# A gated convolution block on one core: a listed order of work against one made by a list scheduler, with the windowed convolution in 128x64 tiles

## The chip, the cores and the metric

One core of one Trainium2 chip. The metric is device time in microseconds of the whole program; the kernel before takes 413.35 us, the median of three runs (411.96, 413.48, 413.35).

## What is computed

The input x is 8 sequences of 4224 tokens by 192 channels, float32. Two stages follow each other:

```python
# stage 1: per head (8 heads of 24 channels) a causal window of 7 tokens, weights softmaxed
w = softmax(weight)                                   # 8 x 7
y[b, s, h, :] = sum_k w[h, k] * xpad[b, s + k, h, :]
# stage 2: a gate and two projections
gate = sigmoid(sum_k conv_w[k] * ypad[:, k:k + S, :]) # 5 taps per channel
out = (gate * (y @ w_val)) @ w_out                    # 192 x 192 each
```

The weights `w_val`, `w_out` and `conv_w` arrive as float64 and are turned into float32 on the chip.

## The kernel before

**Blocks and groups.** The host lays the 8 padded sequences out as two streams of 16,936 tokens. Each token block ("step") has 486 or 488 tokens of both streams; there are 35 steps, the last of 380. A group is what the convolution makes at once: 4 steps (two in the first group, one in the last), ten groups (`NJS`, `BLOCKS`).

**Stage 1** runs on TensorE as a matmul with a banded 128x122 matrix per head (`band`): the stationary operand is a 128-token window of x for 128 (segment, channel) pairs, the result 122 tokens of them (`conv_begin`, L294, 424 matmuls in 106 units). Every float32 matmul counts as two instructions in the trace. `conv_end` copies a unit from PSUM to an `e` tile on ScalarE (L309), and a DMA on SP's queue (L313) moves its rows to where stage 2 wants them: channels on partitions, tokens along the row, tiles `x1` (128 channels of each of the two streams, so units 0 and 1) and `x2` (64 channels of both streams, unit 2).

**Stage 2**, per step and for three units: tap 0 on ScalarE into PSUM (L341), four taps on VectorE (L351), sigmoid on ScalarE (L358). The products use float32r in three passes, high part times high, low times high, high times low: the high part is a cast on ScalarE (L373), the low part a subtraction on GpSimd (L376). The product V = `w_val` has parts 12 (128x64 tiles, float32, L422), 21 (64x128 tiles, L431), 11 and 22 (128x128 tiles, L439, L447). VectorE multiplies V into the gate (L469, `gated`), the gated value is split in the same way, and O = `w_out` runs the same four parts. ScalarE copies the three results out (L476) and SP's queue stores them (L480).

**The order.** Every engine's order is written out: `SCHEDULE` lists what one window of two steps does (for instance `T12+0`: tap 2 of unit 1 of this step; `U`, `K`: begin and end of a convolution unit), and `window(n)` walks through it. The code at the end runs 18 convolution units before the first two steps are complete, and a few more in the first windows.

Of the kernel before, what the change touches and what calls it, by code (L numbers as in the profile page):

```python
# [27 lines left out]
NJS = [2] + [4] * 8 + [1]  # L30
# [22 lines left out]

C1, C2 = 16, 8


class Plan:


    def __init__(self, nj):  # L60
        self.nj = nj
        self.segs = (8, 8 if nj % 2 == 0 else 4)
        self.wins = (nj, nj // 2 if nj % 2 == 0 else nj)
        self.rows = (128, 16 * self.segs[1])
        self.off = (0, 128 * nj)
        self.width = 192 * nj
        per = [MB // (WIN * w) for w in self.wins]
        self.units = []
        for h in range(NH):
            for i in range(2):  # L70
                if (h + 1) % per[i] == 0:
                    self.units.append((i, tuple(range(h + 1 - per[i], h + 1))))


PLANS = [Plan(nj) for nj in NJS]
GROUP = [max(1, 4 // nj) for nj in NJS]
# [5 lines left out]
SCHEDULE = """  # L82
    V12+0 T11+0 CG2-1 T04+0 E2-2 O12-1 GL2-1 T12+0 Z2+1 V21+0 T13+0 S2+0 GL0-1 O21-1 CX2+1 T21+1
    CG1-1 T14+0 V22+0 GL1-1 T22+1 V110+0 S0+0 G2+0 V111+0 XL2+1 Z1+1 T23+1 O22-1 CX1+2 G0+0 O110-1
    XL1+1 T24+1 E2-1 O111-1 T11+1 CG0+0 U0 Z0+1 G1+0 U1 T12+1 K0 GL0+0 E0-1 T01+1 U2 K1 T13+1 E1-1
    U3 T02+1 K2 U4 T14+1 K3 T03+1 CG2+0 U5 Z2+2 GL2+0 T04+1 V110+1 K4 T21+2 CG1+0 V111+1 K5 T22+2
    GL1+0 V22+1 Z0+2 T23+2 O22+0 CX1+3 XL1+2 T01+2 O110+0 S2+1 T02+2 O111+0 S0+1 T24+2 V21+1 CX2+2
    T03+2 O21+0 Z1+2 XL2+2 G0+1 V12+1 G1+1 E0+0 CG0+1 O12+0 E1+0 G2+1
"""
SCHEDULE = [re.fullmatch(r"([A-Z]+)(\d*)([+-]\d+)?", t).groups() for t in SCHEDULE.split()]  # L90
SCHEDULE = [(k, a, int(b or 0)) for k, a, b in SCHEDULE]

XW = 768
XBUFS = 8
# [3 lines left out]
def kernel(  # L98
# [17 lines left out]
    op = ctx.enter_context(tc.tile_pool(name="op", bufs=2))
    ps_g = ctx.enter_context(tc.tile_pool(name="ps_g", bufs=2, space=PSUM))
    ps_v = ctx.enter_context(tc.tile_pool(name="ps_v", bufs=6, space=PSUM))

    w0 = cp.tile([128, KW], F32, name="w0")
    scr = [op.tile([128, 3 * MB], F32, tag="ot", name=f"scr_{i}") for i in range(2)]
    scr.append(pp.tile([128, 2, MB], F32, tag="h", name="scr_2").rearrange("p a t -> p (a t)"))
    scr.append(pp.tile([128, 2, MB], F32, tag="l", name="scr_3").rearrange("p a t -> p (a t)"))
    scr_at = [0] * len(scr)

    def scratch(n, i):
        o = scr_at[i]
        scr_at[i] += n  # L130
        return scr[i][:, o : o + n].bitcast(I32)

    raw = {}
    for name, ap, n, i in (("cw", cw, 2 * KG, 0), ("wv", wv, 2 * D, 0), ("wo", wo, 2 * D, 1)):
        t = scratch(2 * n, i)
        raw[name] = t.rearrange("p (n w) -> p n w", w=2), t, ap.bitcast(I32)

    heads = [(g, h) for g in range(NG) for h in range(0, NH, GROUP[g])]
    xtiles, xoff, loaded = {}, {}, [0]
    o = 0  # L140
    for g, h in heads:
        xoff[g, h] = o
        o += WK * PLANS[g].width * GROUP[g]

    def load_x(k=1):
        for _ in range(k):
            i = loaded[0]
            if i == len(heads):
                return
            loaded[0] += 1  # L150
            g, h = heads[i]
            n = PLANS[g].width * GROUP[g]
            t = xin.tile([WK, XW], F32, tag="x", name=f"x_{g}_{h}")
            nc.sync.dma_start(t[:, :n], xw[xoff[g, h] : xoff[g, h] + WK * n].rearrange("(p f) -> p f", f=n))
            for j in range(GROUP[g]):
                xtiles[g, h + j] = t, j * PLANS[g].width

    def load_raw(name):
        nc.sync.dma_start(raw[name][1], raw[name][2])

    RROW = 2 * WIN + KW
    with tc.manual_schedule(engines={ENG.SP}):
        nc.sync.dma_start(w0, hw)
        load_x(2)
        load_raw("cw")
        load_raw("wv")

        one = cp.tile([128, 1], F32, name="one")
        nc.vector.memset(one, 1.0)
        warm = cp.tile([128, 1], F32, name="warm")  # L170
        nc.scalar.activation(warm, one, AF.Exp)
        row = cp.tile([128, RROW], F32, name="row")
        nc.gpsimd.memset(row, 0.0)

        mx = cp.tile([128, 1], F32, name="mx")
        nc.vector.tensor_reduce(out=mx, in_=w0, op=ALU.max, axis=mybir.AxisListType.X)
        w1 = cp.tile([128, KW], F32, name="w1")
        nc.vector.tensor_tensor(out=w1, in0=w0, in1=mx.to_broadcast([128, KW]), op=ALU.subtract)
        w2 = cp.tile([128, KW], F32, name="w2")
        nc.scalar.activation(w2, w1, AF.Exp)  # L180
        warm2 = cp.tile([128, 1], F32, name="warm2")
        nc.scalar.activation(warm2, w2[:, 0:1], AF.Sigmoid)
        sm = cp.tile([128, 1], F32, name="sm")
        nc.vector.tensor_reduce(out=sm, in_=w2, op=ALU.add, axis=mybir.AxisListType.X)
        sm2 = cp.tile([128, 1], F32, name="sm2")
        nc.vector.tensor_scalar(out=sm2, in0=sm, scalar1=1e-9, scalar2=None, op0=ALU.add)
        rs = cp.tile([128, 1], F32, name="rs")
        nc.vector.reciprocal(rs, sm2)
        nc.vector.tensor_tensor(
            out=row[:, WIN - 1 : WIN - 1 + KW], in0=w2, in1=rs.to_broadcast([128, KW]), op=ALU.mult  # L190
        )

        band = cp.tile([WK, NH, WIN], F32, name="band")
        for h in range(NH):
            r = row[16 * h : 16 * h + 1, :]
            src = bass.AP(tensor=r.tensor, offset=r.offset, ap=[list(r.ap[0]), [1, WK], [1, WIN]])
            nc.sync.dma_start(band[:, h, :], src)  # L197
        load_x(2)
        load_raw("wo")
        load_x(3)  # L200
# [386 lines left out]
```

## Time and profile before

| | |
|---|---|
| runs | 411.96, 413.48, 413.35 us, median 413.35 |
| profiled execution | span 411.2 us from its first to its last instruction; a run's own time holds that and 0.8 to 2.3 us around it |
| busy | TensorE 370.8 us, VectorE 350.2, ScalarE 326.3, GpSimd 243.6 |
| DMA | 81.56 MB, mean 198 GB/s |
| TensorE's clock | 0.966 of full speed on average |

A busy time is the union of an engine's instructions; matmuls overlap, so their mean duration is longer than the distance from one to the next. A row's "idle" is the time that the engine stood still just before, with what released it.

### The profile page before, as it was taken

Reading aid. Unit: us, or ns where it says so; the run is one execution under the profiler, and the core shown is the slowest. Engines: PE = TensorE matmul, PEld = TensorE weight load, DVE = VectorE, ACT = ScalarE, POOL = GpSimd, SP = SyncE. Lnnn points to the kernel's source line nnn. Section 1 sums busy time; section 2 is a strip of 40 time slices with the busy share of each in tenths; the row PEclk is TensorE's granted clock in tenths of the full one; section 3 lists DMA queues with packets and bytes.
Section 4 is the critical chain, followed back from the end, with each engine's and each line's share of the span. In section 5 each row is a group of like instructions: output and inputs, shape, how many; then the busy total and the mean of one; then the engine's idle time right before and its main releaser. Section 6 shows DMA issues by size and latency. Waiting matters only on the chain.

```text
span 411.2 us, 7389 instructions
## 1 busy us (share of the span) xinstructions
PE 370.8 (90%) x2458; PEld 296.5 (72%) x2458; DVE 350.2 (85%) x572; ACT 326.3 (79%) x568; POOL 243.6 (59%) x190
## 2 busy tenths in 40 slices
PE   1766367999999999999999999999999999888896
PEld 0666345979797979797979797979797877646564
DVE  4250199979699999999999999999999999999991
ACT  3232538988899899898989898989898989977874
POOL 0220146746377666766676667666757675858582
PEclk9887769999999999999999999999999999999899
DMA  6899990699999996969796969696977824212033
GB/s 140 200 240 225 238 234 20 192 216 276 236 240 291 269 251 236 238 221 214 247 241 217 269 190 266 189 260 208 242 214 200 214 79 135 86 73 120 29 146 129
DMA packets 38806, 81.56 MB, mean 198 GB/s; under 512 B 7280, under 2 KB 25072, under 8 KB 38768
## 3 DMA queue, kind: packets, MB, share of 16 engines
q1 hardware_dynamic: 38512, 80.59, 73.9%
q0 software_dynamic: 256, 0.50, 0.6%
q8 instruction: 19, 0.31, 0.3%
q14 instruction: 19, 0.16, 0.1%
HBM read 28.33 MB, written 26.01 MB: 132 GB/s over the span
## 4 chain that ended last, share of the span: by engine, by line
PE 74%; DMA 10%; DVE 7%; SPq 2%; issue 2%; ACT 2%; POOL 1%; DVEq 0%; POOLq 0%
PE pc L294 21%; PE po L439 10%; PE pv L439 9%; PE pv L431 6%; PE pv L422 6%; PE po L422 6%; PE pv L447 5%; PE po L431 5%; PE po L447 5%; DMA x<-xw 5%; DVE pg L351 4%; DMA x<-e 4%; SPq L197 2%; DVE g L469 2%; POOL pl L376 1%
## 5 line engine op out<-in xcount | busy, mean ns | idle before, releaser
L351 DVE SCALAR_TENSOR_TENSOR pg<-x,cwt,pg 128x486 f32<-128x486 f32 (+2 forms) x315 | 219.6, 723 | 16.2 <-ACT pg L341 13.6
L376 POOL TENSOR_TENSOR pl<-g,ph 128x488 fp32r<-128x488 f32 (+2 forms) x105 | 128.2, 1230 | 99.1 <-ACT ph L373 98.9
L376 POOL TENSOR_TENSOR xl<-x,xh 128x972 fp32r<-128x972 f32 (+3 forms) x70 | 112.4, 1618 | 44.5 <-ACT xh L373 44.5
L294 PE MATMUL pc<-band,x 128*128 128x122 f32 (+1 forms) x848 | 108.2, 289 | 19.6 <-DMA band<-row 9.0
L294 PEld LDWEIGHTS pc<-band,x 128*128 128x128 f32 (+1 forms) x848 | 105.5, 203 | 23.4 <-issue 13.2
L309 ACT COPY e<-pc 128x488 f32<-128x488 f32 x106 | 60.4, 575 | 44.2 <-PE pc L294 25.8
L341 ACT ACTIVATE pg<-x,cwt 128x488 f32<-128x488 f32 (+2 forms) x105 | 70.3, 669 | 14.7 <-DVE g L351 14.7
L351 DVE SCALAR_TENSOR_TENSOR g<-x,cwt,pg 128x488 f32<-128x488 f32 (+2 forms) x105 | 75.0, 715 | 0.7
L469 DVE TENSOR_TENSOR g<-pv,g 128x488 f32<-128x488 f32 (+2 forms) x105 | 67.0, 657 | 9.2 <-PE pv L422 4.2
L373 ACT CAST ph<-g 128x488 fp32r<-128x488 f32 (+2 forms) x105 | 62.6, 597 | 2.6 <-DVE g L469 2.2
L476 ACT COPY ot<-po 128x488 f32<-128x488 f32 (+2 forms) x105 | 59.0, 565 | 6.0 <-PE po L431 3.6
L358 ACT ACTIVATE g<-g 128x486 f32<-128x486 f32 (+2 forms) x70 | 54.8, 808 | 8.6 <-DVE g L351 8.6
L373 ACT CAST xh<-x 128x972 fp32r<-128x972 f32 (+1 forms) x70 | 55.3, 791 | 4.7 <-DMA x<-e 4.2
L422 PE MATMUL po<-g,wof 128*64 128x244 f32 (+2 forms) x280 | 35.0, 368 | 3.4 <-DVE g L469 3.4
L422 PE MATMUL pv<-x,wvf 128*64 128x244 f32 (+2 forms) x280 | 35.9, 378 | 0.5 <-DVE g L469 0.5
L439 PE MATMUL pv<-xl,wvh 128*128 128x486 f32 (+2 forms) x70 | 27.6, 395 | 9.0 <-POOL xl L376 9.0
L422 PEld LDWEIGHTS po<-g,wof 128*64 128x64 f32 x280 | 20.1, 136 | 12.7 <-DVE g L469 4.2
L422 PEld LDWEIGHTS pv<-x,wvf 128*64 128x64 f32 x280 | 18.4, 138 | 14.1 <-issue 4.9
L439 PE MATMUL po<-pl,woh 128*128 128x486 f32 (+2 forms) x70 | 27.4, 391 | 1.2 <-POOL pl L376 1.2
L439 PE MATMUL pv<-xh,wvh 128*128 128x486 f32 (+2 forms) x70 | 28.2, 403 | 0.0
L439 PE MATMUL po<-ph,woh 128*128 128x486 f32 (+2 forms) x70 | 26.8, 383 | 1.3 <-ACT ph L373 1.3
L439 PE MATMUL pv<-xh,wvl 128*128 128x486 f32 (+2 forms) x70 | 26.8, 383 | 0.0
(67 smaller groups left out, 380.6 us busy)
## 6 DMA issues: line engine op xcount, KB each, us to landing
x<-xw SPq DMA_DIRECT2D x70, 384.0 KB, 8.0
x<-e SPq DMA_DIRECT2D x64, 244.0 KB, 7.9
out<-ot SPq DMA_DIRECT2D x18, 729.0 KB, 7.1
out<-ot SPq DMA_DIRECT2D x16, 732.0 KB, 4.6
x<-e SPq DMA_DIRECT2D x72, 122.0 KB, 7.9
out<-ot SPq DMA_DIRECT2D x3, 190.0 KB, 1.9
band<-row SPq DMA_DIRECT2D x8, 61.0 KB, 5.3
x<-e POOLq DMA_DIRECT2D x8, 61.0 KB, 8.1
```

The source lines that it names most:

```text
L294: nc.tensor.matmul(pc[:m, c : c + WIN], lhsT=t[:, o + w * m : o + w * m + m], rhs=band[:, h, :], start=True, stop=True,)
L309: nc.scalar.copy(e[:m, :n], opened.pop((g, u))[:m, :n])
L341: nc.scalar.mul(acc, unit_view(n, i, 0), cwt[:, i // 2, 0:1])
L351: nc.vector.scalar_tensor_tensor(out=dst, in0=unit_view(n, i, k), scalar=cwt[:, i // 2, k : k + 1], in1=acc, op0=ALU.mult, op1=ALU.add,)
L358: nc.scalar.activation(v, v, AF.Sigmoid)
L373: nc.scalar.copy(h, x)
L376: nc.gpsimd.tensor_tensor(out=l, in0=x, in1=h.bitcast(F32), op=ALU.subtract)
L422: nc.tensor.matmul(acc[p, c], lhsT=self.w.f[:, W12 : W12 + 64], rhs=self.x1[:, q, c], start=first and i == 0, stop=not first and i == 1,)
L431: nc.tensor.matmul(acc, lhsT=a[p, W21 : W21 + 128], rhs=b[p], start=first and i == 0, stop=not first and i == 2,)
L439: nc.tensor.matmul(acc, lhsT=a[:, W11 : W11 + 128], rhs=b[:, q], start=first and i == 0, stop=not first and i == 2,)
L469: nc.vector.tensor_tensor(out=v, in0=pvs.pop((n, q)), in1=v, op=ALU.mult)
L476: nc.scalar.copy(ot[:, q * m : (q + 1) * m], pos.pop((n, q)))
```

## The change

The kernel is written anew around the same arithmetic. Nothing of the order is listed any more: the program adds operations with an engine, a cost in ns, dependencies and a priority to a `Scheduler`, whose `run()` makes the order of every engine before the kernel is emitted. Its core, cut:

```diff
-NJS = [2] + [4] * 8 + [1]
-SCHEDULE = """ V12+0 T11+0 CG2-1 T04+0 E2-2 O12-1 ...
+RUNS = [122, 244] + [488] * 16 + [332]
+SPLIT = {122: [240], 244: [484], 488: [486, 486], 332: [484, 176]}
+class Scheduler:
+    SWITCH, STICK = 100, 3500
+    RATE, FLIGHT, LAND = 270.0, 1300, 900
...
+                        k = o.prio + (self.STICK if e == "PE" and mode not in (None, o.mode) else 0)
...
+FULL_OUT = (0,)
+POOL_GATE = (0,)
```
```diff
 convolution of one unit
-    nc.tensor.matmul(pc[:m, c : c + WIN], lhsT=t[:, o + w * m : o + w * m + m], rhs=band[:, h, :], ...)
+    for w, (a, n) in enumerate(cc):
+        for h, P in enumerate(HALVES):
+            nc.tensor.matmul(
+                at(pc)[P, j * run + a : j * run + a + n],
+                lhsT=t[:, off + 128 * w + 64 * h : off + 128 * w + 64 * h + 64],
+                rhs=band[:, head(c, q, h), :n], start=True, stop=True)
+    ns = sum(2 * (0.80 * n + 5) for _, n in cc) * len(qs)
 part 11 of the product O, unit 0 (q in FULL_OUT)
+    nc.tensor.matmul(at(acc[q])[:, :m], lhsT=wf[kind][:, W11 : W11 + 128], rhs=full_x(q), ...)
 gate of unit 0 (q in POOL_GATE)
-    nc.vector.tensor_tensor(out=v, in0=pvs.pop((n, q)), in1=v, op=ALU.mult)
+    nc.scalar.copy(at(vb)[:, :m], at(pv[q])[:, :m])
+    nc.gpsimd.tensor_tensor(out=gate(q), in0=at(vb)[:, :m], in1=gate(q), op=ALU.mult)
 start of the program
-    8 small DMAs make the bands from one row
+    the bands are loaded (500 KB) and exponentiated on ScalarE; 7 matmuls of zeros go first on TensorE
```

In words: (a) groups ("superblocks") of two steps, the first two small (240 and 484 tokens), 19 of them, 36 steps, the last of 176 tokens; the second product's weights are decoded between the first steps' taps. (b) Each convolution matmul has a 128x64 stationary operand, and two heads fill the two column halves of a bank: 848 matmuls, L491. (c) The gate of unit 0 is multiplied on GpSimd from a copy that ScalarE makes (L660, L663); the cast and the subtraction that split it are gone, since (d) part 11 of O for unit 0 is one float32 matmul (L620). (e) Sigmoids are three per step instead of two or three. New lines: taps L578, first split L555 (cast) and L559, gates L669, second split L680 and L684, products L599 (12), L612 (21), L623 (11), L628 (22), copies L505 and L697, row moves L518, loads L475.

**TensorE, middle of the program.** Before (po and pv: results of O and V; pc: a unit of the convolution):

```order
L439 MATMUL po_1_768<-pl_698,woh 128x488
L294 MATMUL pc_9_821<-band,x_6_381 128x122 x4
L294 MATMUL pc_10_829<-band,x_7_591 128x122 x4
L294 MATMUL pc_11_841<-band,x_6_381 128x122 x2
L294 MATMUL pc_11_841<-band,x_7_591 128x122 x2
L294 MATMUL pc_0_854<-band,x_0_593 128x122 x4
L294 MATMUL pc_1_868<-band,x_1_634 128x122 x4
L294 MATMUL pc_2_881<-band,x_0_593 128x122 x2
L294 MATMUL pc_2_881<-band,x_1_634 128x122 x2
L439 MATMUL pv_0_890<-xh_651,wvh 128x488
L439 MATMUL pv_0_890<-xh_651,wvl 128x488
```

All 24 convolution matmuls of two steps stand together, between 128x128 parts. Now (yl, yh, xl, xh: splits of x; ph, pl, ga: the gated value, `bank` any PSUM bank):

```order
L491 MATMUL bank_110<-band,xin_65 64x122 x8
L491 MATMUL bank_109<-band,xin_65 64x122 x8
L599 MATMUL bank_111<-xa_78,wfV 64x242 x2
L599 MATMUL bank_111<-xa_78,wfV 64x244 x2
L628 MATMUL bank_111<-yh_85,whV 128x486
L628 MATMUL bank_111<-yh_85,wlV 128x486
L628 MATMUL bank_111<-yl_86,whV 128x486
L491 MATMUL bank_113<-band,xin_66 64x122 x8
L623 MATMUL bank_112<-xh_83,whV 128x486
L623 MATMUL bank_112<-xh_83,wlV 128x486
L623 MATMUL bank_112<-xl_84,whV 128x486
L620 MATMUL bank_110<-ga_91,wfO 128x486
```

The convolution now stands in pieces of 8 to 24 matmuls, and in these 12 rows the tile form changes three times (128x64, 128x128, 128x64, 128x128). Counted over the whole order, the tile form changes 182 times; before it was 76. Float32 is followed by float32r within 128x128 tiles 29 times, before 15. The last convolution stood 249 rows before TensorE's end, now 108.

**SP's queue, start of the program** (loads x or xin, row moves from e). Before:

```order
L197 DMA band_120<-row_103 128x1x122 x8
L154 DMA x_0_4_129<-xw 128x768
L154 DMA x_0_6_131<-xw 128x768
L159 DMA scr_1_87<-wo 128x768
L154 DMA x_1_0_134<-xw 128x768
L154 DMA x_1_1_136<-xw 128x768
L154 DMA x_1_2_138<-xw 128x768
L313 DMA x1_0_176<-e_0_0_183 16x8x244 x2
L313 DMA x1_0_176<-e_0_1_192 16x8x244 x2
L154 DMA x_1_3_207<-xw 128x768
L154 DMA x_1_4_209<-xw 128x768
L313 DMA x1_0_176<-e_0_3_216 16x8x244 x2
```

Now:

```order
L518 DMA xb0_80<-e0_68 16x4x61 x2
L518 DMA xa0_77<-e1_69 32x4x122
L475 DMA xin3_64<-xw 128x1024
L475 DMA xin4_65<-xw 128x1024
L475 DMA xin5_66<-xw 128x1024
L518 DMA xb1_81<-e2_70 16x4x122 x4
L518 DMA xa1_78<-e3_71 32x4x244
L518 DMA xa1_78<-e4_72 32x4x244
L475 DMA xin6_67<-xw 128x1024
L475 DMA xin0_61<-xw 128x1024
L475 DMA xin1_62<-xw 128x1024
L440 DMA ot0_105<-wo 128x768
```

The rows of the first small superblock are moved (first two rows) before the loads of the third; those loads (xin3 to xin5) then stand ahead of the second superblock's row moves, and the fourth's (xin6, xin0, xin1) ahead of the third's (xb0, xa0).

**GpSimd, from step 4's split on.** Before (xl: low part of x, pl: of the gated value):

```order
L376 TENSOR_TENSOR xl_4_776<-x_1_261,xh_4_775 128x488
L376 TENSOR_TENSOR xl_652<-x_1_260,xh_651 128x976
L376 TENSOR_TENSOR pl_819<-g_3_667,ph_818 128x486
L376 TENSOR_TENSOR pl_3_879<-g_3_668,ph_3_878 128x486
L376 TENSOR_TENSOR pl_819<-g_3_667,ph_818 128x486
L376 TENSOR_TENSOR xl_802<-x_1_260,xh_801 128x2x486
L376 TENSOR_TENSOR xl_5_950<-x_1_261,xh_5_949 128x486
```

Now (gate multiplications are the rows of L663):

```order
L559 TENSOR_TENSOR xl0_84<-xa0_77,xh0_83 128x2x486
L559 TENSOR_TENSOR xl1_88<-xa0_77,xh1_87 128x2x486
L559 TENSOR_TENSOR yl0_86<-xb1_81,yh0_85 128x486
L663 TENSOR_TENSOR ga2_95<-va0_107,ga2_95 128x486
L684 TENSOR_TENSOR pl20_100<-gb2_96,ph20_99 128x486
L684 TENSOR_TENSOR pl10_98<-ga2_95,ph10_97 128x486
L559 TENSOR_TENSOR xl0_84<-xa1_78,xh0_83 128x2x486
L663 TENSOR_TENSOR ga0_91<-va1_108,ga0_91 128x486
```

The multiplication of the gate (ga) stands in the queue behind the splits of later steps, which wait for row moves.

## Rows read from the trace of the kernel before

**Rows 1.** the page: span, then busy time of each engine, share of the span, instructions

```profile
span 411.2 us, 7389 instructions
...
PE 370.8 (90%) x2458; PEld 296.5 (72%) x2458; DVE 350.2 (85%) x572; ACT 326.3 (79%) x568; POOL 243.6 (59%) x190
```

**Rows 2.** stretches: span, busy us of five engines (instructions), PE clock, DMA share, GB/s

```profile
20.00:30.00 10.00, 6.82 (x47) 6.35 (x47) 5.40 (x15) 3.14 (x6) 2.17 (x4) 0.84 1.07 255
50.00:60.00 10.00, 6.23 (x25) 4.07 (x27) 9.75 (x15) 3.74 (x6) 5.27 (x3) 0.54 1.07 220
360.00:380.00 20.00, 17.15 (x96) 10.92 (x94) 19.82 (x32) 15.68 (x26) 14.44 (x11) 1.00 0.22 92
...
157.90:177.87 19.97, 19.97 (x142) 16.35 (x142) 19.34 (x31) 18.29 (x33) 14.27 (x11) 1.00 0.83 230
```

**Rows 3.** PE in order of time, steady part: start us, us, line, operation, count

```profile
157.73 5.51 PE L294 MATMUL pc<-band,x 128*128 128x122 f32 x48
163.01 0.47 PE L439 MATMUL pv<-xh,wvh 128*128 128x488 f32 x1
163.31 0.38 PE L439 MATMUL pv<-xh,wvl 128*128 128x488 f32 x1
163.53 0.38 PE L439 MATMUL pv<-xl,wvh 128*128 128x488 f32 x1
...
170.37 0.99 PE L422 MATMUL pv<-x,wvf 128*64 128x242 f32 x8
171.19 0.99 PE L422 MATMUL po<-g,wof 128*64 128x244 f32 x8
172.11 0.49 PE L431 MATMUL pv<-xh,wvh 64*128 64x486 f32 x2
172.44 0.38 PE L431 MATMUL pv<-xh,wvl 64*128 64x486 f32 x2
...
173.33 0.38 PE L431 MATMUL po<-pl,woh 64*128 64x488 f32 x2
173.63 0.49 PE L447 MATMUL pv<-xh,wvh 128*128 128x486 f32 x1
173.96 0.39 PE L447 MATMUL pv<-xh,wvl 128*128 128x486 f32 x1
...
188.35 0.38 PE L431 MATMUL po<-pl,woh 64*128 64x486 f32 x2
188.66 1.05 PE L422 MATMUL pv<-x,wvf 128*64 128x244 f32 x8
189.54 0.99 PE L422 MATMUL po<-g,wof 128*64 128x242 f32 x8
```

**Rows 4.** groups by line, whole run: busy us, mean ns, idle before

```profile
L376 POOL TENSOR_TENSOR pl<-g,ph 128x488 fp32r<-128x488 f32 (+2 forms) x105 | 128.2, 1230 | 99.1 <-ACT ph L373 98.9
...
L294 PE MATMUL pc<-band,x 128*128 128x122 f32 (+1 forms) x848 | 108.2, 289 | 19.6 <-DMA band<-row 9.0 <-DMA x<-xw 7.3 <-ACT e L309 3.1
...
L469 DVE TENSOR_TENSOR g<-pv,g 128x488 f32<-128x488 f32 (+2 forms) x105 | 67.0, 657 | 9.2 <-PE pv L422 4.2 <-ACT g L358 2.1 <-PE pv L431 1.6
```

**Rows 5.** head: first block of DVE, PE in order of time; a DMA issue, median landing

```profile
49.75 2.26 DVE L351 SCALAR_TENSOR_TENSOR pg<-x,cwt,pg 128x486 f32<-128x486 f32 x3 [8.90 <-ACT pg L341]
...
53.77 0.77 PE L439 MATMUL pv<-xl,wvh 128*128 128x486 f32 x1 [7.28 <-POOL xl L376]
...
71.62 4.57 PE L294 MATMUL pc<-band,x 128*128 128x122 f32 x39
...
x<-e SPq DMA_DIRECT2D x64, 244.0 KB, 7.9
```

**Rows 6.** tail: PE, DVE and ACT in order of time

```profile
337.78 4.09 PE L294 MATMUL pc<-band,x 128*128 128x122 f32 x32
...
403.15 0.55 DVE L469 TENSOR_TENSOR g<-pv,g 128x380 f32<-128x380 f32 x1 [0.39 <-PE pv L422]
...
407.83 0.47 ACT L476 COPY ot<-po 128x380 f32<-128x380 f32 x1 [0.19 <-PE po L439]
```

More of the change, by code (lines that the diff above doesn't have):

```diff
@@ L46 @@
 assert _s == TOTAL
-FLAT = max(s + t for s, t in zip(STARTS, TOKS)) + KW - 1
 N = len(STEPS)
-LAST = N - 1
+TM = max(p.toks for p in SUPERS)
+FLAT = max(p.start + p.toks for p in SUPERS) + WK
 AT = [3 * sum(s[2] for s in STEPS[:n]) for n in range(N + 1)]
[L54 to L72, printed above, removed]
@@ L75 @@
[L75 to L88, printed above, removed]
@@ L89, with head, __init__ @@
[L89 to L94, printed above, removed]
+def head(c, q, half):
+    return 2 * q + half if c == 0 else (q if half == 0 else q + 4)
+class Buf:
+    __slots__ = ("pool", "users", "slot")
+    def __init__(self, pool):
+        self.pool, self.users, self.slot = pool, 0, None
+class Op:
+    __slots__ = ("eng", "ns", "emit", "deps", "prio", "mode", "bufs", "left", "outs", "at", "end", "kb", "ready", "seq", "tag", "chain")
@@ L118 @@
[L118 to L190, printed above, removed]
-        )
[L193 to L200, printed above, removed]
@@ new lines, with at, small, cast_ns @@
+    banks = [pp.tile([128, 512], F32, name=f"bank{i}") for i in range(8)]
+    slots["pv"] = banks[:6]
+    slots["pg"] = banks[6:]
+    def at(b):
+        return slots[b.pool][b.slot]
+    def small(n):
+        return 0.72 * n + 105
+    def cast_ns(n):
+        return 0.823 * n + 100
+    band = sb("band", [WK, NH, WIN])
+    hwt = sb("hwt", [128, NH, KW])
+    w1 = sb("w1", [128, NH, KW])
+    mx = sb("mx", [128, NH])
+    nmx = sb("nmx", [128, NH])
+    sm = sb("sm", [128, NH])
+    rs = sb("rs", [128, NH])
@@ new lines, with decode @@
+    t2 = sc.add("tsig", "ACT", 1500, lambda o: nc.scalar.activation(warm[:, 1:2], warm[:, 0:1], AF.Sigmoid), exps, P0 + 30)
+    ZN = 7
+    bz = sc.buf("pv")
+    zs = []
+    for i in range(ZN):
+        zs.append(
+            sc.add(
+                "zm", "PE", 900,
+                lambda o: nc.tensor.matmul(at(bz), lhsT=zero[:, :128], rhs=zero, start=True, stop=True),
+                (z2,), P0 + i, "F", (bz,),
+            )
+        )
+    def decode(raw, n, bufs, dep, prio, tag):
+        lo, hi = (raw.rearrange("p (n w) -> p n w", w=2)[:, :, i] for i in range(2))
@@ new lines, in decode, with put @@
+        cost = (360, 360, 360, 360, 580, 580, 580, 360, 580)
+        d = dep
+        for i, (f, c) in enumerate(zip(steps, cost)):
+            d = sc.add(f"{tag}{i}", "DVE", c, f, (d,) if not isinstance(d, tuple) else d, prio + i, None, bufs)
+        pr = ta.bitcast(F32), res
+        def put(dst, p0, p1, c0, c1, ns, i):
+            return sc.add(
+                f"{tag}p", "DVE", ns,
+                lambda o: v.tensor_tensor(out=dst, in0=pr[0][p0:p1, c0:c1], in1=pr[1][p0:p1, c0:c1], op=ALU.add),
+                (d,), prio + 20 + i, None, bufs,
+            )
@@ new lines @@
+    PO = -6000.0
+    put, do = decode(raw_o, NO, (boot_x1, boot_x2, boot_ot), (ld_wo, dv), PO, "do")
+    fo = weight("O", put, 0, zw)
+    ho = sc.add("whO", "ACT", 420, lambda o: nc.scalar.copy(wh["O"], wf["O"][:, :NR]), fo + [zw[1]], PO + 60)
+    lo = sc.add(
+        "wlO", "DVE", 500,
+        lambda o: v.tensor_tensor(out=wl["O"], in0=wf["O"][:, :NR], in1=wh["O"].bitcast(F32), op=ALU.subtract), (ho,), PO + 60,
+    )
+    full = {"V": fv[0], "O": fo[0]}
+    full1 = {"V": fv, "O": fo}
+    split = {"V": lv, "O": lo}
@@ L356, in sigmoid @@
-    def sigmoid(n, i):
-        v = g1s[n] if i < 2 else g2s[n]
-        nc.scalar.activation(v, v, AF.Sigmoid)
-    def halves(d, pool, tag, n, i):
-        if (n, i) not in d:
-            m = STEPS[n][2]
-            if i == 0:
-                d[n, i] = [pool.tile([128, 2, MB], F32R, tag=t, name=f"{tag}{t}_{n}")[:, :, :m] for t in ("h", "l")]
-            else:
-                d[n, i] = [pool.tile([128, MB], F32R, tag=t, name=f"{tag}{t}_{n}")[:, :m] for t in ("h2", "l2")]
-        return d[n, i]
@@ L522, with layout @@
+    order = sc.run()
+    if REPORT is not None:
+        REPORT(order)
+    with tc.manual_schedule(engines={ENG.SP, ENG.PE, ENG.Activation, ENG.DVE, ENG.Pool}):
+        for o in order:
+            o.emit(o)
+REPORT = None
+def layout(x, weight, moe_w_val, moe_conv_w, moe_w_out):
     import numpy as np
-    import concourse.bacc as bacc
-    from concourse.bass_utils import run_bass_kernel_spmd
     f = np.float32
@@ L576 @@
         kernel(tc, *args)
-    r = run_bass_kernel_spmd(nc, [arrays], core_ids=[0])
+    return nc
+def kernel(x, weight, moe_w_val, moe_conv_w, moe_w_out):
+    import numpy as np
+    from concourse.bass_utils import run_bass_kernel_spmd
+    arrays, perm = layout(x, weight, moe_w_val, moe_conv_w, moe_w_out)
+    r = run_bass_kernel_spmd(build(arrays), [arrays], core_ids=[0])
     got = r.results[0]["out"]
-    full = np.empty((NS, TOTAL, D), f)
+    full = np.empty((NS, TOTAL, D), np.float32)
     for n, (g, o, m) in enumerate(STEPS):
-        a = STARTS[g] + o
+        a = SUPERS[g].start + o
         blk = got[:, AT[n] : AT[n + 1]].reshape(128, 3, m)
```

781 lines of the change are left out of this document (511 added, 270 removed).

## The prediction

> **What bounds the kernel now.** First the page: TensorE is busy for 370.8 of 411.2 us, VectorE for 350.2 [rows 1], so either could be the bound, and an average won't say which. So I read by stretches. In the steady part two steps take 19.97 us; TensorE is busy in all of it at full clock (1.00), VectorE in 19.34, ScalarE in 18.29, GpSimd in 14.27 [rows 2]. The reader should see that there TensorE sets the pace and VectorE is 3% behind it, so relieving VectorE alone buys at most a little.
>
> Then TensorE's instructions in order of time, by the distance of starts and not by duration, since they overlap [rows 3]. 48 convolution instructions take 163.01 - 157.73 = 5.28 us, 0.110 each (a matmul is two). Eight instructions of part 12 in 128x64 tiles take 171.19 - 170.37 = 0.82, 0.1025 each for 243 columns. A 128x128 float32r pass takes 163.53 - 163.31 = 0.22, and so does a pair of 64x128 ones. So V and O cost, per step, 0.82 + 3 x 0.22 + 6 x 0.22 + 3 x 0.22 = 3.46 us each. Two steps: 4 x 3.46 + 5.28 = 19.12, and 0.85 us are missing from 19.97. They stand where the tile form changes: from 171.19, 0.82 + 0.22 should end at 172.23, and the second pair starts at 172.44 (0.21 lost); 64x128 to 128x128 loses 173.96 - 173.33 - 0.44 = 0.19; 64x128 to 128x64 loses 189.54 - 188.35 - 0.22 - 0.82 = 0.15; float32 to float32r without a new form 0.08 (163.01 to 163.31, less 0.22). I take 0.185 per change of form. TensorE's whole work at full clock is then 848 instructions [rows 4] x 0.110 = 93.3, plus 34.85 steps of 486 tokens x 6.92 = 241.1, plus 76 x 0.185 = 14.1, plus 15 x 0.08 = 1.2: 350 us.
>
> Last the two ends. VectorE's first tap starts at 49.75 us, TensorE waits 7.28 us before 53.77 and works without a gap only from about 71.62 [rows 5]; the DMA engines are full meanwhile (share 1.07, 255 and 220 GB/s) and the granted clock falls to 0.54 between 50 and 60, near the lower of its two levels [rows 2]. At 71.62 TensorE has done 72 convolution matmuls (15.8), V and O of two steps (13.8) and some changes of form, about 31 us. So 319 remain, to 390.6, and the end is at 411.2: 20.6 us are lost at the tail. The rows say how: the last convolution ends at 341.8 [rows 6], after which VectorE is at 19.82 of 20 us while TensorE has 17.15 to do [rows 2].
>
> **The change, part by part.** Times are against the profiled execution's span of 411.2 us; the median of the runs, 413.35, lies 2.1 above it, and I add 1.5 at the end.
>
> *Convolution in 128x64 tiles.* 848 matmuls, 1696 instructions; narrower ones in the small superblocks make them worth 1674 of 122 columns (102,072 columns over 122, twice). No row shows this shape with its two halves in turn. Below, the pairs could stream as part 12 does: 0.1025 x 122 / 243 = 0.0515 each, 86.1 us. Above, two halves could cost what one full matmul does, 0.055 each: 92.1 us. I take the middle, 0.0535 and 89.5 us, since part 12 is the same tile form but the short stretch hides a weight load less well: **-3.8** (-7 to -1). That the halves don't overlap at all is a rival below. A rule speaks against this part: the Trainium skill (TensorEngine Tiling (Array Packing), section Performance Considerations) states an overhead of about 60 cycles on each matmul. At 2.4 GHz that is, by estimate, 0.025 us; taking it out of 0.1025, halving the rest and adding it again gives 0.064 and 107 us, 18 more than my term. The rows hint otherwise, as 243 columns in two halves leave no visible surplus over 0.22 for 488 columns of a full pass, but no run here has the short shape.
>
> *Part 11 of O in float32 for unit 0.* Three passes, 0.66 us a step, go. One float32 matmul of 486 columns comes: 0.82 by part 12 (two halves of 243 columns are 4 x 0.1025 x 2), 0.88 by the convolution (2 x 0.110 x 486 / 122). With 0.85: 34.85 x 0.19 = **+6.6** (5.6 to 7.6). The cast and the subtraction that it saves lie on ScalarE and GpSimd, beside TensorE.
>
> *Changes of form.* The new order has 182 instead of 76, and 29 instead of 15 from float32 to float32r: 106 x 0.185 + 14 x 0.08 = **+20.7** (16 with 0.15, 23 with 0.21). The source plans 0.100 for one; the rows say twice that. TensorE's work becomes 350 - 3.8 + 6.6 + 20.7 = **373 us**, 10.6 a step instead of 10.0.
>
> *Gate of unit 0 on GpSimd, sigmoids apart, copies.* VectorE loses 0.64 us a step (67.0 / 105 [rows 4]): from 9.67 (19.34 / 2) to 9.0. GpSimd gets a multiplication for a subtraction of 1.22 (128.2 / 105 [rows 4]), ScalarE a copy for a cast and about 0.1 for one more sigmoid. All of this is covered by TensorE's 10.6, so I cost it at **nothing**. If TensorE were 1.5 us a step faster than I think, ScalarE's 9.15 and VectorE's 9.0 would be the floor.
>
> *Start.* Steps 0 and 1 together are 1.5 ordinary steps; steady work begins when the third superblock's rows have landed. By SP's order 8.4 MB come before that: bands and weights 1.3, loads of four superblocks 4.45, row moves of three 2.6. At 237 GB/s (mean of 255 and 220 [rows 2]) and with 1.2 us to the first: **37 us** (34 with 255 GB/s, 43 with 200). By then TensorE has done the convolutions of four superblocks, 136 x 0.107 = 14.6, V of two steps 5.1 and some 15 changes of form 2.8: 22.5 us, and 350.5 remain. The matmuls of zeros lie in the wait for the first loads and cost nothing there; if the bands are ready before them, 2 us.
>
> *End.* The last convolution now stands 108 rows before the end, some three steps of work, instead of 249. VectorE's 9.0 against TensorE's 7.9 there loses 3 us; the chain behind the last gate was 411.2 - 403.7 = 7.5 [rows 6], less for 176 tokens, so 6. Together **9** (6 to 14) for 20.6.
>
> **Sum:** 37 + 350.5 + 9 = 396.5 of span, 398 us as a time. In short, TensorE gets 23 us more work and the two ends give back 37.
>
> **The rivals.**
>
> (A) *The changes of form cost less than in the rows*, since a 128x64 piece of 8 often stands where TensorE waits anyhow, and the halves stream at 0.0515. Then 10 of the 20.7 go, and 3.4 of the convolution, and 34 us at the start instead of 37: 381.5. For it: a drain costs nothing in a wait. Against: in the steady part there is no wait now.
>
> (B) *GpSimd's queue holds up the gate*: slower. The multiplication of unit 0 stands behind the low parts of x for a later step, and those wait for row moves, whose median landing is 7.9 us [rows 5]. If they land late, the gate is late, O's float32 part behind it is late, and TensorE, in order, stands still; its clock may fall as between 50 and 60. Each of 17 superblocks would lose d us; above d = 0.9 the gain of 15 is gone, and d = 1.5 gives 398 + 25 = 423. For it: the planner counts 270 GB/s where rows show 220 to 255, and a wrong cost upsets a fixed order on all engines. Against: the old order had the same split ahead of pl on GpSimd and TensorE didn't wait there; and TensorE's longer step gives everything else 6% more time.
>
> (C) *The halves don't pay*: any s us per convolution instruction above 0.0535 adds 1674 x that. At 0.0625 the gain is gone (+15, 413); if the halves ran one after the other at 0.1025, +82 and 480. By the Trainium skill's figure above, 0.064, the time would be 416. For it: no row shows two convolution-sized halves. Against: part 12 overlaps.
>
> (D) *The start gives nothing*, as row moves still queue behind the loads: 37 becomes 50, and 411 comes out, no change.
>
> **How the numbers follow.** Forecast, 387 to 409: 0.52. (A) 0.20. (B) 0.14, most of it slower. (C) 0.08, half of it far above. (D) 0.06. The range 377 to 423 leaves out about 0.04 of (A) and 0.1 of (B) and (C). 0.5% is 2.1 us, about what a measurement of this kernel can tell from no change. Faster by more: 0.52 + 0.20 + 0.02 of (B) = 0.74; within: 0.08, from (D) and the low ends of (B) and (C); slower: 0.18.
>
> **What would show it.** Right: in the middle TensorE at 100% and full clock, two steps in about 21.3 us; 0.05 to 0.055 between convolution starts; 0.15 to 0.21 lost at each change of form; VectorE's first tap near 14 us, TensorE gapless from about 37; under 7 us between VectorE's last gate and the end. Wrong: gaps on TensorE in the middle, released by GpSimd (B); convolution starts 0.06 or more apart (C); two steps in 20 us or less (A). A time above 411 or below 381 would mean that one of these terms, not its rounding, is off.

## The result, and the profile after

The changed kernel takes 403.17 us (median of four runs, 402.81 to 404.77), the kernel before 413.42 beside it: ratio 0.975, interval 0.970 to 0.980. Faster, 5 us above the forecast of 398 and inside its range. Some runs of the kernel before fall into a slower state; every ratio in this document compares fast runs only.

The page of the changed kernel answers to [rows 1] with its span and the busy time of each engine, and to [rows 5] with the median landing of a row move:

```profile
span 401.4 us, 9387 instructions
PE 383.8 (96%) x3330; PEld 276.7 (69%) x3330; DVE 343.0 (85%) x550; ACT 329.7 (82%) x626; POOL 246.1 (61%) x197
...
xa<-e SPq DMA_DIRECT2D x64, 244.0 KB, 3.0
```

TensorE is busy 13 us longer in a span that is 10 us shorter, so the time came from its idle ends. The stretches show where (columns as in [rows 2]):

```profile
30.00:40.00 10.00, 10.00 (x125) 7.75 (x121) 9.58 (x16) 7.71 (x16) 6.47 (x5) 1.00 0.81 287
40.00:50.00 10.00, 4.02 (x21) 1.79 (x21) 9.97 (x13) 6.56 (x12) 7.34 (x5) 0.79 0.67 232
50.00:60.00 10.00, 10.00 (x48) 6.96 (x48) 7.23 (x14) 4.99 (x12) 3.27 (x3) 0.70 0.26 103
100.00:380.00 280.00, 280.00 (x2476) 203.71 (x2472) 247.95 (x378) 245.00 (x457) 180.39 (x133) 1.00 0.56 211
380.00:411.00 31.00, 17.46 (x111) 10.64 (x109) 13.81 (x28) 14.24 (x33) 12.51 (x12) 0.96 0.21 81
```

TensorE has no gap from 100 to 380 at full clock, VectorE is down to 89% there, and there is a hole between 40 and 50. TensorE's waits in the first 60 us name what fills it (what waited, for whom: us in all, times, longest; the 5.4 us end at 18.8, before the hole). The last line is the instruction that ends the longest wait in the hole:

```profile
PE bank L599 <- DMA xa<-e: 5.4, 1, 5.4
PE bank L599 <- DVE wfO L411: 3.5, 1, 3.5
PE bank L623 <- POOL xl L559: 1.6, 1, 1.6
...
49.94 1.07 PE L599 MATMUL bank<-ga,wfO 128*64 128x120 f32 x8 [3.50 <-DVE wfO L411]
```

The 3.5 us are for the decoded weights of O; VectorE, which decodes them, is busy for 9.97 of these 10 us. The middle, in order of time, answers to [rows 3]:

```profile
203.21 2.72 PE L491 MATMUL bank<-band,xin 128*64 128x122 f32 x48
205.76 0.99 PE L599 MATMUL bank<-xa,wfV 128*64 128x242 f32 x8
206.68 1.08 PE L620 MATMUL bank<-ga,wfO 128*128 128x486 f32 x2
207.22 0.76 PE L628 MATMUL bank<-ph,whO 128*128 128x486 f32 x1
207.81 0.38 PE L628 MATMUL bank<-ph,wlO 128*128 128x486 f32 x1
...
223.46 0.48 PE L612 MATMUL bank<-ph,whO 64*128 64x486 f32 x2
223.79 0.38 PE L612 MATMUL bank<-ph,wlO 64*128 64x486 f32 x2
224.00 0.39 PE L612 MATMUL bank<-pl,whO 64*128 64x486 f32 x2
224.32 2.72 PE L491 MATMUL bank<-band,xin 128*64 128x122 f32 x48
```

48 convolution instructions take 2.55 us, 0.053 each (forecast 0.0535), and these two steps 224.32 - 203.21 = 21.11 (forecast 21.3). Averaged over 100 to 370 us, by the starts of equal matmuls two steps apart, two steps take 20.85. A change of form shows as 224.32 - 224.00 = 0.32 where 0.22 would do, and 0.33 instead of 0.22 behind the first pass: 0.1 on either side.

**Work done, by time.** To compare runs I weigh TensorE's instructions by their steady spacing (convolution 0.053, part 12 0.1025, float32 0.41, the float32r passes 0.2165 a row, 0.1085 for each of a pair), without changes of form, and count each once, by its start. The narrow pieces at the two ends count as full ones, alike in all rows, so the columns compare kernels and are no absolute amounts. The expectations below have some of these figures (39.9, 33.3, 35.1 and 351 us) 3 to 5% higher: there an instruction on the edge of a window stood in both windows, and part 12 was weighed with 0.108.

| run | changes of form | work done at 60 us | done from 60 to 380 | left at 380, and the time it took |
|---|---|---|---|---|
| changed kernel | 182 | 32.3 | 293.0 | 17.0 in 21.4 |
| sticky | 122 | 33.5 | 301.1 | 7.6 in 10.3 |
| earlyo | 186 | 38.2 | 291.9 | 12.1 in 20.3 |
| both0 | 191 | 29.3 | 290.5 | 16.2 in 24.0 |
| dvegate | 163 | 32.5 | 295.9 | 13.8 in 17.5 |
| split3 | 231 | 29.1 | 275.3 | 31.6 in 41.6 |
| st_eo | 119 | 39.5 | 298.7 | 4.0 in 7.6 |
| st_pg | 123 | 33.3 | 297.7 | 11.3 in 15.0 |
| st_eo_fo | 130 | 37.6 | 292.5 | 6.0 in 9.6 |

### The profile page after: what moved, and what is told of

It reads as the page before. It is cut to its first block, busy times and chain, and to the rows that moved or that the text cites. A ratio compares the mean times of both kernels' runs of the same rounds, so it can differ in the third digit from the quotient of the medians.

```text
span 401.4 us, 9387 instructions
## 1 busy us (share of the span) xinstructions
PE 383.8 (96%) x3330; PEld 276.7 (69%) x3330; DVE 343.0 (85%) x550; ACT 329.7 (82%) x626; POOL 246.1 (61%) x197
## 4 chain that ended last, share of the span: by engine, by line
PE 84%; DVE 5%; ACT 3%; issue 2%; POOL 1%; DMA 1%; ACTq 1%; SPq 1%; POOLq 0%; DVEq 0%
PE bank L491 22%; PE bank L623 17%; PE bank L599 14%; PE bank L612 12%; PE bank L628 11%; PE bank L620 7%; DVE bank L578 3%; PE bank L378 2%; DMA xb<-e 1%; ACTq L518 1%; ACT ot L697 1%; ACT ga L584 1%; ACT bank L572 1%; DVE ga L578 0%; ACT ph L680 0%
## 5 line engine op out<-in xcount | busy, mean ns | idle before, releaser
L578 DVE SCALAR_TENSOR_TENSOR bank<-xa,cwt,bank 128x486 f32<-128x486 f32 (+3 forms) x216 | 147.1, 708 | 10.0 <-ACT bank L572 7.4
L559 POOL TENSOR_TENSOR xl<-xa,xh 128x972 fp32r<-128x972 f32 (+3 forms) x36 | 74.0, 2058 | 68.5 <-ACT xh L555 58.6
L491 PEld LDWEIGHTS bank<-band,xin 128*64 128x64 f32 x1696 | 89.4, 138 | 15.2 <-issue 6.6
L491 PE MATMUL bank<-band,xin 128*64 128x122 f32 (+2 forms) x1696 | 99.4, 271 | 0.2 <-ACT ot L697 0.2
L578 DVE SCALAR_TENSOR_TENSOR bank<-xb,cwt,bank 128x486 f32<-128x486 f32 (+3 forms) x108 | 75.3, 708 | 3.8 <-ACT bank L572 1.9
L697 ACT COPY ot<-bank 128x486 f32<-128x486 f32 (+3 forms) x108 | 56.3, 555 | 24.3 <-PE bank L599 10.8
L505 ACT COPY e<-bank 128x488 f32<-128x488 f32 (+2 forms) x107 | 59.6, 573 | 9.0 <-PE bank L491 6.9
L684 POOL TENSOR_TENSOR pl<-ga,ph 128x486 fp32r<-128x486 f32 (+3 forms) x36 | 43.4, 1205 | 27.1 <-ACT ph L680 26.7
L663 POOL TENSOR_TENSOR ga<-va,ga 128x486 f32<-128x486 f32 (+3 forms) x36 | 43.2, 1201 | 25.8 <-ACT va L660 14.0
L572 ACT ACTIVATE bank<-xa,cwt 128x486 f32<-128x486 f32 (+3 forms) x72 | 48.9, 679 | 4.6 <-DVE gb L578 4.6
L578 DVE SCALAR_TENSOR_TENSOR ga<-xa,cwt,bank 128x486 f32<-128x486 f32 (+3 forms) x72 | 50.4, 700 | 1.4
L684 POOL TENSOR_TENSOR pl<-gb,ph 128x486 fp32r<-128x486 f32 (+3 forms) x36 | 43.2, 1200 | 9.5 <-ACT ph L680 9.5
L559 POOL TENSOR_TENSOR yl<-xb,yh 128x486 fp32r<-128x486 f32 (+3 forms) x36 | 40.8, 1134 | 8.7 <-ACT yh L555 8.0
L584 ACT ACTIVATE ga<-ga 128x486 f32<-128x486 f32 (+3 forms) x72 | 43.5, 604 | 0.4 <-DVE ga L578 0.4
L572 ACT ACTIVATE bank<-xb,cwt 128x486 f32<-128x486 f32 (+3 forms) x36 | 23.7, 659 | 20.8 <-DVE ga L578 20.4
L599 PE MATMUL bank<-xa,wfV 128*64 128x242 f32 (+3 forms) x288 | 35.4, 367 | 5.4 <-DMA xa<-e 5.4
L599 PE MATMUL bank<-ga,wfO 128*64 128x242 f32 (+3 forms) x288 | 37.1, 377 | 3.5 <-DVE wfO L411 3.5
L669 DVE TENSOR_TENSOR ga<-bank,ga 128x486 f32<-128x486 f32 (+3 forms) x36 | 23.2, 645 | 19.8 <-ACT ga L584 19.6
L555 ACT CAST xh<-xa 128x972 fp32r<-128x972 f32 (+3 forms) x36 | 36.1, 1002 | 2.2 <-DMA xa<-e 2.2
L620 PE MATMUL bank<-ga,wfO 128*128 128x486 f32 (+3 forms) x72 | 37.0, 599 | 0.0
L623 PE MATMUL bank<-xh,whV 128*128 128x486 f32 (+3 forms) x72 | 34.9, 485 | 0.6 <-ACT xh L555 0.6
L599 PEld LDWEIGHTS bank<-ga,wfO 128*64 128x64 f32 x288 | 18.0, 138 | 20.7 <-issue 8.9
```

The costliest lines, as they stand in the source:

```text
L491: nc.tensor.matmul(at(pc)[P, j * run + a : j * run + a + n], lhsT=t[:, off + 128 * w + 64 * h : off + 128 * w + 64 * h + 64], rhs=band[:, ...
L505: o2 = lastev[g] = sc.add(f"e{g}.{k}", "ACT", small(n), lambda o, n=n, pc=pc, eb=eb: nc.scalar.copy(at(eb)[:, :n], at(pc)[:, :n]), (o1,), ...
L559: nc.gpsimd.tensor_tensor(out=s[2 * c + 1], in0=views(n)[c], in1=s[2 * c].bitcast(F32), op=ALU.subtract)
L572: lambda o, n=n, i=i, pg=pg, m=m: nc.scalar.mul(at(pg)[:, :m], part(n, i, 0), cwt[:, i // 2, 0:1]),
L578: v.scalar_tensor_tensor(out=acc if k < KG - 1 else gate(i), in0=part(n, i, k), scalar=cwt[:, i // 2, k : k + 1], in1=acc, op0=ALU.mult, o ...
L584: sig[i] = sc.add(f"s{n}.{i}", "ACT", 0.823 * m + 110, lambda o, i=i, gate=gate: nc.scalar.activation(gate(i), gate(i), AF.Sigmoid), (d, t ...
```

## The experiments

Twelve kernels were measured in three groups: sticky, earlyo, conv128, both0; then dvegate, st_pg, st_eo, bigfirst; then split3, st_eo_fo, st_eo_big, z3. The kernel before had medians of 416.2, 417.0 and 417.4 us beside them and 413.4 beside the changed kernel, with single runs from 408 to 426, so between groups a difference of under 1% is not certain from times alone; there I go by the table.

**sticky: fewer changes of form.**

```diff
-    SWITCH, STICK = 100, 3500
+    SWITCH, STICK = 200, 25000
```

> The planner is told that a change of tile form costs 200 ns (not 100) and that TensorE stays in a form up to a priority gap of 25000 (not 3500). The order then has 122 changes of form instead of 182, the work is the same. Theory P (TensorE sets the pace from about 50 us on, and each change costs 0.185 us that nothing hides): 60 x 0.185 = 11 less, 392 us, and two steps in the middle in about 19.9 us instead of 21.1. Rival S (changes lie in waits anyhow, or an order with fewer of them makes the other engines late): 403 us or more, with gaps on TensorE.

392.98 us (ratio 0.948, 0.941 to 0.956). 60 changes fewer save about 10 us, 0.17 each. The middle shows it alone: from 60 to 380 us TensorE idles for 0.2 us in both runs, and with 97 changes instead of 145 it gets 8.1 us more work done, 0.17 for each again. So the forecast's price, 0.185, was right to a tenth, against rival A's half of it. Two steps take some 20.3 us on average for the changed kernel's 20.85; the expectation had 19.9 for 21.1, twice that step.

**earlyo: the weights of O earlier.** In the changed kernel their load waits for V's high part, and their decoding has a late priority.

```diff
-    ld_wo = dma("wo", ..., (hv,), 0, (boot_ot,), 393)
-    PO = -6000.0
+    ld_wo = dma("wo", ..., (ld_wr,), PW + 1, (boot_ot,), 393)
+    PO = P0 + 170.0
```

> The weights of the second product are loaded right after those of the first and decoded before and between the taps of the first step, not of the second and third. Theory H (the late start, TensorE's gap between 45.7 and 49.9 us and the low clock behind it, comes from this decode, whose instructions took up to 1.98 us beside GpSimd's subtractions and 0.57 without): gap and low clock go, 4 to 8 us less, 396 to 399 us, and the decode instructions take 0.36 to 0.57 us again. Rival (VectorE bounds the start whatever its order, 6 us of decode only stand elsewhere): 402 to 404 us.

402.53 us (ratio 0.972, 0.964 to 0.979): the rival's number, yet the hole is gone; the last line is TensorE's last wait before 60 us:

```profile
40.00:50.00 10.00, 10.00 (x89) 6.89 (x87) 9.89 (x16) 9.50 (x19) 9.24 (x8) 1.00 0.48 168
...
380.00:411.00 31.00, 13.06 (x82) 7.97 (x78) 12.91 (x27) 11.32 (x26) 6.64 (x8) 0.89 0.15 57
...
37.46 0.62 PE L599 MATMUL bank<-ga,wfO 128*64 128x120 f32 x6 [1.01 <-DVE ga L669]
```

By the table 5.9 us are won by 60 us and 1.1 given back in the middle. From 380 on less work is left (12.1 against 17.0), but it takes nearly as long, 20.3 against 21.4: another 3.8 lost. TensorE's longest wait at that end is for the gate on GpSimd, and GpSimd's for a sigmoid:

```profile
PE bank L620 <- POOL ga L663: 2.7, 1, 2.7
...
POOL ga L663 <- ACT ga L584: 5.0, 2, 3.6
```

So the gate on GpSimd holds TensorE up there, as in rival B, but once, at the end, and behind a late sigmoid instead of late row moves. The hole cost what was forecast for it and was worth filling only with an order whose end keeps up (st_eo, below).

**conv128: the convolution as before, the rest as changed.** One 128x128 matmul stands for each pair of halves and uses the first head's band for both heads; the second head's band is left out.

```diff
-  for h, P in enumerate(HALVES):
-      nc.tensor.matmul(at(pc)[P, ...], lhsT=t[:, off + 128*w + 64*h : ... + 64], rhs=band[:, head(c, q, h), :n], ...)
+  nc.tensor.matmul(at(pc)[:, ...], lhsT=t[:, off + 128*w : off + 128*w + 128], rhs=band[:, head(c, q, 0), :n], ...)
```

> The convolution's pairs of 128x64 matmuls are replaced by one 128x128 matmul each, which uses the band of the pair's first head for both heads: the second head's part of the computation is changed, the order is kept. 424 matmuls instead of 848. Theory P: 848 instructions of 0.110 instead of 1696 of about 0.053 (+3), 195 changes of form instead of 182 (+2.4), 43 steps from float32 to float32r instead of 29 (+1.1): about +6, 409 us. Rival C (the halves cost more than they stream): below 403 us.

412.51 us (ratio 0.996, 0.992 to 1.000) against 403.17: the halves gain rather than cost, and rival C falls. 3.8 for the convolution, 13 more changes at 0.17 and 14 more steps from float32 to float32r at 0.08 give 7; the other 2 are not accounted for.

**both0, dvegate, split3: two parts undone, together and one by one.**

```diff
-FULL_OUT = (0,)
-POOL_GATE = (0,)
+FULL_OUT = ()      # both0, split3
+POOL_GATE = ()     # both0, dvegate
```

> Unit 0 goes back to what the kernel before did: gate on VectorE, split into high and low part, three passes of part 11 in O; the planner orders this anew (191 changes of form). Theory P: TensorE gets 34.85 x 0.25 = 8.7 less in matmuls (0.91 measured for the float32 one, 0.66 for three passes), 2.3 less from float32 to float32r, 1.7 more in changes of form: 9 less, 394 us. Rival V (the relief of VectorE by 0.64 us a step is what keeps TensorE fed): VectorE has 9.6 us a step, it binds where the order is uneven, 403 us or more.

> The gate of O's unit 0 back on VectorE, as the other units have it; the scheduler then makes 163 form changes instead of 182. VectorE gets 36 multiplications of 0.65 us, 23 us more (343 to 366 of some 400), GpSimd 44 fewer. Theory P (TensorE paces the kernel, the gate's engine is worth nothing in itself): 19 fewer form changes of 0.15 to 0.17, 400 us (399 to 402). Rival V (VectorE is so near its limit that the taps come late, at the end above all, where TensorE would wait for the last units): 403 to 407.

> The changed kernel with O's unit 0 split in three float32r passes instead of the float32 pass, nothing else; the scheduler then makes 231 form changes instead of 182. Theory P (TensorE paces, each change costs 0.13 to 0.17 us): 7.5 us less matmul work, 6.4 to 8.3 more for 49 changes, 403 us (401.5 to 404.5). Rival C (form changes cost little, and the fewer-changes kernel gained from its order in another way): 396 to 398.

| us (changes of form) | unit 0 in float32 | three passes |
|---|---|---|
| gate on GpSimd | 403.17 (182) | 422.18 (231) |
| gate on VectorE | 399.95 (163) | 405.48 (191) |

dvegate came out as P said, 400. The three passes did not: 6 us less work, and 5.5 slower with the gate on VectorE, 19 slower with it on GpSimd, slower even than the kernel before (ratio 1.015, 1.009 to 1.020). For both0 against dvegate the table adds up: 3.2 lost by 60 us, 5.4 in the middle, 4.1 more at the end (24.0 - 16.2 against 17.5 - 13.8), less 6.1 of work: 6.6; the spans differ by 6.5. In the middle TensorE doesn't wait in either run; there 28 more changes of form at 0.17 are 4.8 of the 5.4. For split3 the stretch and TensorE's waits from 60 to 400 us show a cost that I had at nothing:

```profile
100.00:240.00 140.00, 136.14 (x1186) 98.12 (x1185) 116.89 (x178) 123.06 (x232) 103.05 (x78) 1.00 0.57 211
...
PE bank L628 <- ACT va L660: 3.8, 4, 0.9
PE bank L623 <- ACT ot L697: 2.8, 4, 0.7
PE bank L628 <- DVE ga L669: 1.1, 4, 0.3
```

ScalarE's copy of V for GpSimd's gate (va), its copies of the output and VectorE's gates come late, and TensorE, in order, waits: 7.7 us. Against the changed kernel split3 loses 3.2 by 60 us, 17.7 in the middle and 5.6 at the end, for 6.1 less work: 20.4, near the 20.2 of the spans (421.6 and 401.4). Of the middle's 17.7 these waits are 7.7, and its 39 more changes there at 0.17 are 6.6; the rest is not accounted for. So what the float32 part is worth was not in my sum at all: it cost TensorE 6 us and spared unit 0 a cast on ScalarE and a subtraction on GpSimd between gate and matmul. That this shorter chain is why the scheduler gets by with fewer changes and waits is my reading; no run here separates it from the order that the scheduler happens to make.

**st_pg: the gate moved at an equal number of changes** (the sticky constants, and POOL_GATE = ()).

> The scheduler's fewer form changes together with the gate of O's unit 0 back on VectorE; 123 form changes, one more than with the gate on GpSimd, so that here the gate is moved at an equal number of changes. TensorE's work is the same 351 us without the changes. Theory P (the gate's engine is worth nothing while TensorE paces): 393 us (391.5 to 394). Rival V (VectorE, 23 us more at some 94% busy, paces the middle or the end): 395 to 400.

396.97 us (ratio 0.966, 0.959 to 0.974), 4 more than sticky: rival V. The middle of st_pg, then that of sticky:

```profile
100.00:380.00 280.00, 279.06 (x2481) 210.39 (x2477) 266.34 (x416) 237.64 (x438) 155.88 (x113) 1.00 0.58 209
```

```profile
100.00:380.00 280.00, 279.79 (x2465) 211.64 (x2463) 252.81 (x389) 250.01 (x468) 189.76 (x141) 1.00 0.58 208
```

VectorE is busy for 266 of 280 us. TensorE's waits after 60 us, 2.6 in all, name VectorE's gates and ScalarE's copies of the output, up to 0.7 each. By the table 3.4 us less work is done in the middle, of which only 0.9 shows as more waiting, and the end loses 1.0 more. So the gate on GpSimd is worth nothing in the changed kernel, and about 4 us where there are few changes of form; that these changes give VectorE the time it needs is argued, not shown.

**st_eo, st_eo_fo: the two gains together, and without the float32 part.**

> The scheduler's fewer form changes (119) together with the early load and decoding of O's weights. Early O weights alone had 39.9 us of TensorE's matmul work done at 60 us, against 33.3 in the changed kernel and 35.1 with the fewer form changes alone; it then lost 4 of these 6.6 us at the end, where the last units' taps on VectorE and gate on GpSimd came late, and 1.7 in the middle. Theory E (the end's loss belongs to that one order of the work, not to the early start): 4.8 us off the 393 of the fewer form changes, 388 (386.5 to 389.5). Rival T (VectorE's last taps set the end, so that an earlier start is given back there): 391.5 to 393.5.

389.56 us (389.14 to 390.09; ratio 0.949, 0.942 to 0.956), just above E's upper edge: 3.4 below sticky. At 60 us it is 6.0 ahead of sticky; 2.4 go in the middle and 0.9 at the end.

> The scheduler's fewer form changes and the early O weights, and O's unit 0 split in three float32r passes like the other units instead of the float32 pass. Form changes 130 instead of 119. TensorE's matmul work falls from 351 to 343.5 us; VectorE has nothing more to do, ScalarE and GpSimd get 18 casts of 0.6 and 18 subtractions of 1.2 us. Theory P (TensorE paces, the float32 pass is only a cost to it): 7 us less work, 1.5 more for the changes, 384 us (382.5 to 386). Rival V (the split's chain, gate to cast to subtraction to matmul, is longer than gate to matmul, and TensorE waits for it): 388 to 392.

390.86 us (388.95 to 391.39; ratio 0.938, 0.933 to 0.944), inside V's range and far from P's 384. The 6.1 us of work saved come back as 6.2 in the middle, where TensorE waits for 4.3 us instead of 1.8, and 1.9 at the start. The ratios say otherwise (0.938 against 0.949), but they hang on the kernel before, whose runs differ between the groups; the traces, both at full clock in the middle, put st_eo_fo's span 2.0 us above st_eo's.

**bigfirst, st_eo_big: no small first superblocks.**

```diff
-RUNS = [122, 244] + [488] * 16 + [332]
+RUNS = [488] * 17 + [208]
```

> Superblocks of 488 columns from the first on, with the short one of 208 at the end, in place of 122 and 244 first and 332 last; the scheduler then makes 171 changes of tile form on TensorE instead of 182. In the changed kernel the first tap started at 16.6 us with TensorE idle for 5.4 us ahead of it, but TensorE also stood still at 46 to 50 us for the decoded O weights, and ran at a clock of 0.70 to 0.79 there. Theory S (small first superblocks shorten the start): every step of the first chain is four times as wide, the first rows come back later, and steady work starts 4 to 8 us later; 407 us (405 to 410). Rival W (the weights' loads and decoding set the start whatever the superblocks are): nothing is lost at the start, 11 fewer form changes of about 0.15 give 1.7; 401.5 (400 to 403.5).

> The scheduler's fewer form changes and the early O weights, with superblocks of 488 from the first on and 208 last; 113 form changes instead of 119. With O's weights out of the way, the first superblock's own chain should be what sets the start. Theory S (small first superblocks then pay): the first rows come later and steady work starts 3 to 6 us later, 393 us (391 to 396). Rival W (they pay nothing here either): 0.8 less for the changes and some for fewer, wider pieces, 388.5 (387 to 390).

400.05 us (ratio 0.973, 0.962 to 0.985) and 389.07 (387.88 to 390.26; ratio 0.935, 0.929 to 0.940): rival W both times. The small superblocks gain nothing that shows; in bigfirst TensorE stands still for the O weights as well (2.8 us). st_eo_big and st_eo, which I can't tell apart, are the fastest of all: some 3.4% below the changed kernel, from constants, two priorities and a dependency (in st_eo_big the sizes of the superblocks too).

**z3: three pairs of matmuls on zeros instead of seven** (ZN = 3).

> Half of the matmuls on zeros at the start left out (3 pairs instead of 7), the program order otherwise the same. In the changed kernel the first zeros run at 0.57 us each up to 9.3 us, the first convolution follows at once at 9.2 to 13.4, and then TensorE idles for 5.4 us. Theory K (they keep the clock up for the first convolution): at half the clock 80 small matmuls take 2 us more and the first taps come later, 405 (404 to 406.5). Rival N (the convolution waits for its input anyway and the idle time behind it takes up any difference): 403 (402 to 404).

401.69 us (ratio 0.965, 0.959 to 0.971), a little below N's range; K falls: from 0 to 10 us the granted clock is 1.00 in both runs. The first convolution of z3, then that of the changed kernel:

```profile
8.19 1.62 PE L491 MATMUL bank<-band,xin 128*64 128x61 f32 x32 [1.39 <-DMA xin<-xw]
```

```profile
9.22 4.13 PE L491 MATMUL bank<-band,xin 128*64 128x61 f32 x80
```

With seven pairs the convolution stands behind the zeros and not behind its input; with three it starts 1.0 us earlier. The zeros, at nothing in the prediction (2 us if the bands came before them), cost about that.

## Why the prediction was right or wrong, point by point

- **Convolution**, -3.8 from 0.0535 an instruction: 0.053 in the rows. Right, and conv128 shows at least that gain. The 0.064, estimated from the overhead per matmul that the Trainium skill states (TensorEngine Tiling (Array Packing), section Performance Considerations), is not what these rows show.
- **Changes of form**, +20.7 for 106 and 14: right. sticky gives 0.17 for each. (The trace of the kernel before has 80 changes, not 76: four more lie inside its last convolution group, 0.7 us.) The steady pace, 20.85 on average for 21.3, holds work, float32 part and changes together; at 16 pairs of steps it is 7 us better than forecast.
- **Start**, "37 us" with "22.5 us" of work done: this is the step that failed. TensorE is gapless only from 49.94, with some 25 us done by then; that is about 10 us, and the clock of 0.70 from 50 to 60 costs 3 more, as the stretches show. I had reckoned the start from bytes alone. By 40 us the bytes were no longer the limit: the share of the DMA engines from 40 to 50 was 0.67, from 50 to 60 0.26, and row moves landed in 3.0 us (median) instead of 7.9 [rows 5]. What was late was the decoding of O's weights on VectorE, which the sum didn't hold. earlyo shows it: with the weights early, TensorE is gapless from 37.46. VectorE's first tap, forecast near 14 us, came at 16.64, against 49.75 before. Which part of the new order brought it forward (loads, bands, row moves) no run here separates; the small superblocks are not needed for it.
- **End**, 9 us: TensorE is busy for 17.46 of the 21.4 us from 380 to the end, with the narrow last pieces taking longer than their columns. Weighed by columns and with 15 changes of form, as the sum does, it does 15.1 us of work there: 6 are lost, so 3 better. The last gate ends 4.8 us before the end, for a forecast of 6.
- The errors, +13, -7 and -3, add up to 3, near the 4.9 between 401.4 and the forecast 396.5. That the result was nearer than its parts is luck.
- **Gate on GpSimd at nothing**: right for the changed kernel as it stands, by dvegate, which is even 3.2 faster, as its 19 fewer changes at 0.17 would make it. The float32 part as a mere +6.6 was wrong: its work is 6.1, but undone it costs 5 to 19 us, and undone with few changes of form (st_eo_fo) it gives back none of its 6.
- **Rival B** failed on its condition, late row moves: between 60 and 380 us TensorE never waited for GpSimd, and after that 0.6 us for its low parts. A late gate on GpSimd showed only at the end of earlyo, behind a sigmoid. **Rival D** gave 50 us for the start; 50 it was, for another reason.

## What to carry to other kernels

Price a change of tile form from the rows, and give a list scheduler that price: here 60 changes at 0.17 us were as much as the whole change had gained. When an idle start is to shrink, follow every input of the first units to its engine, the decoding of weights too, and not only the bytes. A part that costs the pacing engine can still be a gain by the order that becomes possible around it; undo it alone before calling it a cost.
